# A kernel of convolution and 16 experts: the copy of a page's expert number moves to the head of VectorE's turn

## The chip, the core and the metric

The kernel runs on one core of a Trainium2 chip. The metric is the device time of one execution in microseconds; the time of a kernel is the median of its runs.

The engines are named as in the profile: PE is TensorE (matmuls; PEld its weight loads), DVE is VectorE, ACT is ScalarE, POOL is GpSimd, SP is SyncE, which here only issues DMAs. An engine's sequencer (ACTq, DVEq, SPq) handles what isn't work of the engine itself, such as loading a register from memory.

## The reference

Four sequences of 10048 positions with 128 channels go through a gated long convolution, and the 40192 rows that come out through one of 16 experts each, chosen in two steps (one group of four, then one of its four experts).

```
h = relu(pos_emb @ w1) @ w2 * exp(-0.01 * pos)          # the filter
y = irfft(rfft(x * v, 2*SEQ) * rfft(h, 2*SEQ))[:SEQ]    # a causal convolution of length SEQ
x = x * y                                               # 40192 rows of 128
g = argmax(x @ w_group);  e = argmax(x @ w_expert[g])   # weights: softmax over groups, over experts
out[row] = p_group * p_expert * (relu(x[row] @ w1[g, e]) @ w2[g, e])     # 128 -> 1024 -> 128
```

## The kernel before

The convolution stage takes the first 1,100 us or so, the routing of the rows follows, and the expert stage fills the second half of the execution, from 1250 us on. The change lies in the expert stage.

**Pages.** Routing sorts the rows into pages of 256, each of one expert, and `work` goes through 164 of them in a loop whose body is `turn`. Every matrix is split into a high and a low part (`wh` and `wl`, `xh` and `xl`, `hh` and `hl`), so that a product is three matmuls: high by high, high by low, low by high. The first weights `mw` of all experts stay in SBUF; the second ones, `ws`, come by two DMAs a page.

**A turn** works on five pages at once: it ends page `old`, does the second product of `p0` and the first of `p1`, transposes and splits the rows of `p2`, and begins `p3`, which means: find out its expert and fetch its second weights. The columns of 1024 are taken in blocks of 128, two to a relu, so the relus of a turn are those of blocks 0, 2, 4 and 6; the text calls them hh(0) to hh(6) on ScalarE and hl(0) to hl(6), the low parts, on VectorE. In the code `first(c)` (L1169 to L1171, into `ph`) and `second(c)` (L1188 to L1190, into `py`) are matmuls, `relu(c)` is hh (L1177) and hl (L1178), `high` and `low` are the casts of weights on ScalarE (L1150) and the subtractions on VectorE (L1158; for pages 2 to 41 one of the four is on GpSimd), `turn` of a page is the transpose `px` (L1130), `rows` makes `xh` and `xl`, `leave` copies `py` to `ys` (L1195), `turn_back` transposes it back, `ptm` (L1202), and `weigh` scales it into `os` (L1209).

**Order.** All these instructions are pinned: `k.fix` keeps each behind the one that the code wrote before it on the same engine. So the order of `turn` is the order of each engine. Not pinned are register loads (`value_load`) and the routing of the last batch, from which a step is taken every two turns; a scheduler puts these where it finds room.

**Beginning a page.** `begin` copies the page's expert number from the table `epgi` to a tile `ep` of one element (DVE, L1097), and three sequencers load it into a register: ScalarE's (L1099) and VectorE's (L1100), which address `mw` with it, and SyncE's (L1102), which addresses the two DMAs of `ws` (L1107). `ep` and `ws` have three buffers each.

**GpSimd's transfers.** `fetch` issues the gathers of a page's rows, `xg` (L1114, two a page, up to six pages ahead), the sends of finished rows, `out` (L1214, two a page, with up to 24 pages of `os` waiting), and the scatters of the last batch's list (L836). Lists are read back (`lst`, L1043) and turned into addresses on VectorE (`to` L1047, `of` L1049).

Of the kernel before, what the change touches and what calls it, by code (L numbers as in the profile page):

```python
# [14 lines left out]
I32 = mybir.dt.int32  # L15
# [115 lines left out]
class Kernel:  # L131
# [310 lines left out]
    def filter(self, ctx, ahead, made, folded):  # L442
# [35 lines left out]
        for k0, n in pairs + [(None, None)]:  # L478
            ahead_of, rest = rest, []
            if k0 is not None:  # L480
                o = k0 % 4
                if o == 0:
                    if k0 // 4 >= NBT:
                        bts.append(bp.tile([128, 4, 128], F32, tag="bt", name="bt", bufs=NBT))
                        m = min(4, NB - k0)
                        nc.sync.dma_start(bts[-1][:, :m], d["c_b"][:, k0 : k0 + m])
                    hs = tp.tile([128, 4, 2, 128], F32, tag="hs", name="hs", bufs=3)
                ps = self.dft_positions(k0, n, bts[k0 // 4][:, o:], k0 % 4 > 0)
                t = tp.tile([128, 2, 2, 128], F32, tag="hw", name="ht", bufs=4)


                for i in range(n):
                    cs, sn, mc = (phase[:, k0 + i, x : x + 1] for x in range(3))
                    tt, pp = t[:, i], ps[:, i]
                    whole = i == 0 or k0 % 8 == 0
                    if whole:
                        turn(nc.scalar.activation(tt[:, 0], pp[:, 0], AF.Copy, scale=cs))
                        turn(nc.scalar.activation(tt[:, 1], pp[:, 1], AF.Copy, scale=mc))
                    else:
                        turn(nc.scalar.activation(tt, pp, AF.Copy, scale=cs))  # L500
                    rest.append((whole, hs[:, o + i], pp, sn, tt))
                rest.append((k0, n, o, hs))
# [452 lines left out]
    def work(self, pages):  # L955


        n = len(pages)
        at = lambda i: pages[i] if 0 <= i < n else None
        for p in pages[:XG]:  # L960
            if p.xg is None:
                p.gather()
        if pages:
            pages[0].begin()
        for i in range(-2, n + 1):
            self.fetch(i, at(i + 1 + XG), at(i + 1))
            self.turn(at(i), at(i + 1), at(i + 2), at(i + 3), at(i - 1))
            if i >= 0 and i % EVERY == EVERY - 1:
                next(self.routing, None)
        while self.outs:  # L970
            self.outs.pop(0)()

    def turn(self, p0, p1, p2, p3, old):


        none = Idle()
        p0, p1, p2, p3, old = (p or none for p in (p0, p1, p2, p3, old))
        old.leave()
        p1.high(1, 0)
        p1.first(0)  # L980
        p2.turn()
        p0.second(0)
        p1.low(1, 0)
        p1.relu(0)
        p2.rows()
        p2.high(0, 0)
        old.turn_back()
        p0.second(1)
        p2.low(0, 0)
        old.weigh()  # L990
        p1.first(2)
        p0.second(2)
        p0.second(3)
        p1.relu(2)
        p2.high(0, 1)
        p1.high(1, 1)
        p2.low(0, 1)
        p1.low(1, 1)
        p1.first(4)
        p0.second(4)  # L1000
        p0.second(5)
        p1.relu(4)
        p3.begin()
        p1.first(6)
        p0.second(6)
        p0.second(7)
        p1.relu(6)
# [78 lines left out]
class Page:  # L1086
    def __init__(self, k, q):
        self.k, self.q = k, q
        self.to = self.of = self.weight = self.xg = None
        self.wh, self.wl, self.hh, self.hl, self.ph = ({}, {}), ({}, {}), [], [], {}  # L1090

    def begin(self):

        k, nc = self.k, self.k.nc
        ep = k.sp.tile([1, 1], I32, tag="ep", name="ep", bufs=3)
        k.tc.keep_in_program_order(
            nc.vector.tensor_copy(ep, k.pages.expert(self.q))  # L1097
        )
        self.ea = nc.scalar.value_load(ep, min_val=0, max_val=NE - 1)  # L1099
        self.ed = nc.vector.value_load(ep, min_val=0, max_val=NE - 1)  # L1100

        es = nc.sync.value_load(ep, min_val=0, max_val=NE - 1)  # L1102
        self.ws = []
        for half in range(2):
            ws = k.sp.tile([128, 512], F32, tag=f"ws{half}", name="ws", bufs=3)
            src = k.d["m_w2"][:, ds(es, 1), half * 512 : half * 512 + 512]
            k.tc.keep_in_program_order(nc.sync.dma_start(ws, src.rearrange("p e f -> p (e f)")))  # L1107
            self.ws.append(ws)
# [202 lines left out]
```

## Time and profile before

| | |
|---|---|
| median of 3 runs | 2534.3 us (2530.7 to 2542.32) |
| the profiled execution | 2529.75 us, span 2528.0 us |
| TensorE | 2053.1 us busy (81%), granted clock 0.912 in the mean |
| VectorE | 1719.8 us (68%) |
| GpSimd | 1500.5 us (59%) |
| ScalarE | 1347.5 us (53%) |
| turns 0 to 21 of the expert stage | 1261.3 to 1422.5 us |
| turns 22 to 31 | 1422.5 to 1593.8 us |
| turns 32 to 40 | 1593.8 to 1653.9 us |
| the 120 turns behind them | 1653.9 to 2501.3 us |

The shares are of the whole span and so mix stages with different limits. The profile counts the work of an engine as busy, not the work of its sequencer: a register load on ScalarE's sequencer holds back the next instruction of ScalarE, and shows there as idle time. Matmul durations overlap, so the distance between two starts, not the duration, is what a matmul costs. The granted clock is 1.00 at the full 2.4 GHz.

### The profile page before, as it was taken

How to read it: one execution, taken by the hardware profiler on the slowest of the kernel's cores; microseconds unless marked ns; L12 is line 12 of the kernel's file. 1: busy time of each engine (PE TensorE's matmuls, PEld its weight loads, DVE VectorE, ACT ScalarE, POOL GpSimd, SP SyncE). 2: the span in 40 equal slices, each digit the busy share in tenths (PEclk: the TensorE clock that was granted, in tenths of full speed). 3: DMA queues.
4: the chain of work that ended last, by engine and by line, in shares of the span. 5: the costliest groups of instructions: out<-in, count | busy, mean ns of one | idle time of the engine just before them, and what ended most of it. 6: DMA issues, size and time to landing. Idle time of an engine off the chain costs nothing.

```text
span 2528.0 us, 53511 instructions
## 1 busy us (share of the span) xinstructions
PE 2053.1 (81%) x18062; PEld 1846.6 (73%) x18062; DVE 1719.8 (68%) x3431; ACT 1347.5 (53%) x3005; POOL 1500.5 (59%) x1496
## 2 busy tenths in 40 slices
PE   9989899729996299813989655899999999999987
PEld 8778777607884187712788555888888888888887
DVE  5787778707797077911788623677777777777776
ACT  6733544305442054401677433677777777777776
POOL 2286016860596607674177777866666666666663
PEclk9999999859997599955999866999999999999999
DMA  4899568405773049521433211333333333333332
GB/s 130 296 271 273 148 202 278 126 9 135 252 234 108 10 140 300 166 62 40 152 109 111 74 49 40 111 117 110 113 113 114 114 113 114 114 113 109 111 109 69
DMA packets 201325, 338.65 MB, mean 134 GB/s; under 512 B 38558, under 2 KB 77185, under 8 KB 201040
## 3 DMA queue, kind: packets, MB, share of 16 engines
q1 hardware_dynamic: 159824, 275.64, 35.3%
q0 software_dynamic: 31712, 43.94, 5.6%
q10 hardware_dynamic: 9504, 15.54, 2.5%
q8 instruction: 146, 2.39, 0.4%
q14 instruction: 139, 1.14, 0.2%
HBM read 282.60 MB, written 53.30 MB: 133 GB/s over the span
## 4 chain that ended last, share of the span: by engine, by line
PE 33%; DVE 23%; issue 22%; ACT 8%; POOL 6%; DMA 4%; ACTq 3%; another core or an unknown queue 1%; SPq 0%; DVEq 0%; POOLq 0%
DVE wl L1158 7%; PE psa L301 4%; DVE hl L1178 3%; ACT wh L1150 3%; PE psb L371 3%; PE ph L1171 2%; DMA xv<-xv_in 2%; PE ph L1170 2%; PE ph L1169 2%; PE pbp L544 2%; ACTq L1099 2%; PE py L1190 2%; ACT ys L1195 2%; PE po L605 2%; PE py L1188 2%
## 5 line engine op out<-in xcount | busy, mean ns | idle before, releaser
L1178 DVE SCALAR_TENSOR_TENSOR hl<-ph,hh 128x512 fp32r<-128x512 f32 x656 | 451.1, 688 | 307.7 <-ACT hh L1177 262.4
L1177 ACT ACTIVATE hh<-ph 128x512 fp32r<-128x512 f32 x656 | 408.1, 622 | 364.6 <-PE px L1130 214.8
L1114 POOL DMA_INDIRECT xg<-xyd,of x328 | 388.6, 1185 | 229.9 <-PE px L1130 160.4
L1214 POOL DMA_INDIRECT out<-os,to x328 | 366.2, 1117 | 148.6 <-ACT os L1209 78.5
L1190 PE MATMUL py<-hh,wl 128*128 128x256 f32 x1312 | 378.5, 289 | 39.4 <-issue 27.0
L1188 PE MATMUL py<-hh,wh 128*128 128x256 f32 x1312 | 405.0, 309 | 0.3 <-issue 0.3
L836 POOL DMA_INDIRECT list<-en,adr x316 | 320.8, 1015 | 109.9 <-issue 88.3
L1169 PE MATMUL ph<-xh,wh 128*128 128x256 f32 x1312 | 377.9, 288 | 3.6 <-ACT xh L1137 2.6
L1170 PE MATMUL ph<-xl,wh 128*128 128x256 f32 x1312 | 377.6, 288 | 2.4 <-issue 2.4
L1171 PE MATMUL ph<-xh,wl 128*128 128x256 f32 x1312 | 377.6, 288 | 1.8 <-issue 1.4
L1189 PE MATMUL py<-hl,wh 128*128 128x256 f32 x1312 | 377.0, 287 | 1.0 <-issue 1.0
L533 POOL TENSOR_TENSOR y<-t 128x256 f32<-128x256 f32 (+1 forms) x160 | 119.4, 746 | 342.6 <-DVE t L532 340.0
L1190 PEld LDWEIGHTS py<-hh,wl 128*128 128x128 f32 x1312 | 257.2, 196 | 41.3 <-issue 28.4
L1169 PEld LDWEIGHTS ph<-xh,wh 128*128 128x128 f32 x1312 | 258.5, 197 | 4.4 <-ACT xh L1137 2.9
L1171 PEld LDWEIGHTS ph<-xh,wl 128*128 128x128 f32 x1312 | 257.8, 196 | 3.8 <-issue 2.9
L1189 PEld LDWEIGHTS py<-hl,wh 128*128 128x128 f32 x1312 | 258.3, 197 | 2.0 <-issue 2.0
L1170 PEld LDWEIGHTS ph<-xl,wh 128*128 128x128 f32 x1312 | 257.9, 197 | 0.7 <-issue 0.7
L1188 PEld LDWEIGHTS py<-hh,wh 128*128 128x128 f32 x1312 | 257.3, 196 | 1.1 <-issue 1.1
L1158 DVE TENSOR_TENSOR wl<-mw,wh 128x512 fp32r<-128x512 f32 x328 | 228.9, 698 | 0.3
L1150 ACT CAST wh<-ws 128x512 fp32r<-128x512 f32 x328 | 213.8, 652 | 12.6 <-remote 6.0
L1158 DVE TENSOR_TENSOR wl<-ws,wh 128x512 fp32r<-128x512 f32 x288 | 200.1, 695 | 23.0 <-ACT wh L1150 5.5
L1150 ACT CAST wh<-mw 128x512 fp32r x328 | 214.8, 655 | 0.0
(228 smaller groups left out, 4300.6 us busy)
## 6 DMA issues: line engine op xcount, KB each, us to landing
ws<-m_w SPq DMA_DIRECT2D x328, 256.0 KB
ht<-hspec SPq DMA_DIRECT2D x156, 256.0 KB
xv<-xv_in SPq DMA_DIRECT2D x131, 288.0 KB
bt<-c_b SPq DMA_DIRECT2D x95, 256.0 KB
bp<-c_bp SPq DMA_DIRECT2D x76, 256.0 KB
xyd<-xy SPq DMA_DIRECT2D x57, 256.0 KB
xo<-x_out ACTq DMA_DIRECT2D x60, 237.0 KB
hspec<-hs SPq DMA_DIRECT2D x19, 512.0 KB
```

The source lines that it names most:

```text
L1114: ins = nc.gpsimd.indirect_dma_start(self.xg[:, h], None, self.src, bass.IndirectOffsetOnAxis(ap=self.of[:, h : h + 1], axis=0), bounds_ch ...
L1150: k.fix(k.nc.scalar.copy(hi, self.matrix(i, half, self.ea)))
L1158: v.tensor_tensor(lo, self.matrix(i, half, self.ed), self.wh[i][half].bitcast(F32), ALU.subtract)
L1169: k.fix(nc.tensor.matmul(ph[:, j], wh, self.xh, start=True, stop=False))
L1170: k.fix(nc.tensor.matmul(ph[:, j], wh, self.xl, start=False, stop=False))
L1171: k.fix(nc.tensor.matmul(ph[:, j], wl, self.xh, start=False, stop=True))
L1177: k.fix(nc.scalar.activation(hh, ph, AF.Relu))
L1178: k.fix(nc.vector.scalar_tensor_tensor(hl, ph, 0.0, hh.bitcast(F32), ALU.max, ALU.subtract))
L1188: k.fix(nc.tensor.matmul(self.py, wh, self.hh[c], start=(c == 0), stop=False))
L1189: k.fix(nc.tensor.matmul(self.py, wh, self.hl[c], start=False, stop=False))
L1190: k.fix(nc.tensor.matmul(self.py, wl, self.hh[c], start=False, stop=(c == NC - 1)))
L1214: ins = k.nc.gpsimd.indirect_dma_start(k.d["out"], bass.IndirectOffsetOnAxis(ap=self.to[:, h : h + 1], axis=0), o[:, h], None, bounds_chec ...
```

## The change

`begin` is cut in two. The copy of the expert number becomes a function `number`, and `turn` calls it for `p3` ahead of everything else; the register loads and the DMAs of `ws` stay in `begin`, at its old place.

```diff
@@ work
         if pages:
+            pages[0].number()
             pages[0].begin()
@@ turn
         p0, p1, p2, p3, old = (p or none for p in (p0, p1, p2, p3, old))
+        p3.number()
         old.leave()
         p1.high(1, 0)
         p1.first(0)
@@ Page
+    def number(self):
+
+        k = self.k
+        self.ep = k.sp.tile([1, 1], I32, tag="ep", name="ep", bufs=3)
+        k.fix(k.nc.vector.tensor_copy(self.ep, k.pages.expert(self.q)))
+
     def begin(self):
 
-        k, nc = self.k, self.k.nc
-        ep = k.sp.tile([1, 1], I32, tag="ep", name="ep", bufs=3)
-        k.tc.keep_in_program_order(
-            nc.vector.tensor_copy(ep, k.pages.expert(self.q))
-        )
+        k, nc, ep = self.k, self.k.nc, self.ep
         self.ea = nc.scalar.value_load(ep, min_val=0, max_val=NE - 1)
         self.ed = nc.vector.value_load(ep, min_val=0, max_val=NE - 1)
```

On VectorE the order before reads so from hl(4) of a steady turn to hl(2) of the next turn:

```order
L1178 SCALAR_TENSOR_TENSOR hl<-ph,hh 128x512
L1097 COPY ep<-epgi_74 1x1
L1100 TENSOR_LOAD ep
L1100 ISA x2
L1178 SCALAR_TENSOR_TENSOR hl<-ph,hh 128x512
L1158 TENSOR_TENSOR wl_27341<-ws,wh_27325 128x512
L1178 SCALAR_TENSOR_TENSOR hl<-ph,hh 128x512
L1138 TENSOR_TENSOR xl<-px,xh 128x256
L1158 ISA
L1158 TENSOR_TENSOR wl_27359<-mw_11895,wh_27351 128x512
L1178 SCALAR_TENSOR_TENSOR hl<-ph,hh 128x512
```

and after the change, in another steady turn, where line numbers are 1 to 4 higher (the first row is hl(4) and hl(6) of the turn in one):

```order
L1162 TENSOR_TENSOR wl_28575<-ws,wh_28571 128x512
L1182 SCALAR_TENSOR_TENSOR hl<-ph,hh 128x512 x2
L1098 COPY ep<-epgi_74 1x1
L1162 TENSOR_TENSOR wl_28680<-ws,wh_28664 128x512
L1182 SCALAR_TENSOR_TENSOR hl<-ph,hh 128x512
L1142 TENSOR_TENSOR xl<-px,xh 128x256
L1162 ISA
L1162 TENSOR_TENSOR wl_28698<-mw_11895,wh_28690 128x512
L1104 TENSOR_LOAD ep
L1104 ISA x2
L1182 SCALAR_TENSOR_TENSOR hl<-ph,hh 128x512
```

The copy stood between hl(4) and hl(6); now it comes behind both, at the head of the next turn and for that turn's page. VectorE's register load (TENSOR_LOAD and two instructions for addresses, ISA) stood right behind the copy and stands now behind the first `wl` from `mw`. ScalarE's steady turn has one order before and after: the load stands behind hh(4) and ahead of hh(6).

On SyncE the load of the last part's list, `lst` with 380 elements, moves. Before, it follows the 33rd load of an expert number and that page's DMAs:

```order
L1102 TENSOR_LOAD ep
L1102 ISA x2
L1107 ISA
L1107 DMA ws<-m_w 128x512
L1107 ISA
L1107 DMA ws<-m_w 128x512
L1043 DMA lst_28642<-list 128x380
```

After the change it stands between the two weight loads of the 42nd:

```order
L1106 TENSOR_LOAD ep
L1106 ISA x2
L1111 ISA
L1111 DMA ws<-m_w 128x512
L1045 DMA lst_28642<-list 128x380
L1111 ISA
L1111 DMA ws<-m_w 128x512
```

With it move the scatters ahead of it: the 79 of the last batch on GpSimd end before the gathers of the 31st page in the order before, and before those of the 37th after; VectorE's two rows of `to` move from the 34th copy to the 42nd. TensorE's order is the same.

## Rows read from the trace of the kernel before

**Rows 1.** Windows of the expert stage: busy time per engine, clock, DMA share.

```profile
core 0: us, PE busy (x) PEld busy (x) DVE busy (x) ACT busy (x) POOL busy (x), PEclk, DMA share, GB/s
1261.30:1422.50 161.20, 142.75 (x1136) 139.35 (x1135) 141.18 (x279) 115.08 (x264) 121.54 (x107) 0.97 0.34 106
1422.50:1593.80 171.30, 91.41 (x523) 85.70 (x522) 53.26 (x95) 55.91 (x120) 134.16 (x130) 0.70 0.18 50
1593.80:1653.90 60.10, 56.49 (x460) 54.65 (x460) 44.50 (x82) 46.83 (x108) 50.30 (x46) 1.00 0.38 120
1653.90:2501.30 847.40, 770.85 (x6248) 746.25 (x6248) 655.89 (x1202) 625.52 (x1440) 552.91 (x472) 1.00 0.36 111
```

**Rows 2.** Tile `ep`, 1653.8 to 2501.4: count, duration (ns) min/median/max, first and last start.

```profile
L1097 DVE COPY ep<-epgi x121: 130/131/133, 1653.9 to 2501.3; 1x1 int32<-1x1 int32 x121
...
L1099 ACTq TENSOR_LOAD <-ep x120: 279/365/389, 1654.1 to 2494.5; - x120
```

**Rows 3.** View of waits, 1653.9 to 2501.3: total us, times, longest.

```profile
ACT hh L1177 <- PE px L1130: 202.5, 111, 2.1
```

**Rows 4.** Timeline of ScalarE in a steady turn: start, duration, then idle time before.

```profile
2000.18 0.60 ACT L1177 ACTIVATE hh<-ph 128x512 fp32r<-128x512 f32 x1 [1.82 <-PE px L1130]
...
2004.73 0.66 ACT L1177 ACTIVATE hh<-ph 128x512 fp32r<-128x512 f32 x1
2007.21 0.60 ACT L1177 ACTIVATE hh<-ph 128x512 fp32r<-128x512 f32 x1 [1.82 <-PE px L1130]
```

**Rows 5.** Timeline of TensorE at the same place.

```profile
2005.21 0.28 PE L1171 MATMUL ph<-xh,wl 128*128 128x256 f32 x1
...
2006.65 0.28 PE L1171 MATMUL ph<-xh,wl 128*128 128x256 f32 x1
2006.77 0.38 PE L1130 MATMUL px<-ident,xg 128*128 128x128 f32 x2
2006.91 0.37 PE L1188 MATMUL py<-hh,wh 128*128 128x256 f32 x1
...
2008.12 0.44 PE L1202 MATMUL ptm<-ident,ys 128*128 128x128 f32 x2 [0.61 <-ACT ys L1195]
```

**Rows 6.** Timeline of VectorE in that turn.

```profile
2000.81 0.69 DVE L1178 SCALAR_TENSOR_TENSOR hl<-ph,hh 128x512 fp32r<-128x512 f32 x1 [1.40 <-ACT hh L1177]
...
2006.31 0.13 DVE L1097 COPY ep<-epgi 1x1 int32<-1x1 int32 x1
2007.84 0.69 DVE L1178 SCALAR_TENSOR_TENSOR hl<-ph,hh 128x512 fp32r<-128x512 f32 x1 [1.40 <-ACT hh L1177]
```

**Rows 7.** Timeline of ScalarE in the turn that begins no page.

```profile
2506.77 1.39 ACT L1177 ACTIVATE hh<-ph 128x512 fp32r<-128x512 f32 x2
```

**Rows 8.** Timeline of TensorE in that turn: its first transpose and the next turn's.

```profile
2503.13 0.44 PE L1202 MATMUL ptm<-ident,ys 128*128 128x128 f32 x2 [0.58 <-ACT ys L1195]
...
2509.16 0.38 PE L1202 MATMUL ptm<-ident,ys 128*128 128x128 f32 x2
```

**Rows 9.** VectorE's sequencer by line L1100 (ns), and VectorE's timeline, around 1306.

```profile
L1100 DVEq TENSOR_LOAD <-ep x1: 304/304/304, 1305.9 to 1305.9; - x1
...
1305.80 0.67 DVE L1158 TENSOR_TENSOR wl<-ws,wh 128x512 fp32r<-128x512 f32 x1
```

**Rows 10.** Timeline of GpSimd in a steady turn.

```profile
2000.40 1.04 POOL L1114 DMA_INDIRECT xg<-xyd,of  x1 [1.36 <-PE px L1130]
2001.75 1.43 POOL L1114 DMA_INDIRECT xg<-xyd,of  x1 [0.30 <-issue]
2003.49 1.23 POOL L1214 DMA_INDIRECT out<-os,to  x1 [0.30 <-ACT os L1209]
2005.02 1.04 POOL L1214 DMA_INDIRECT out<-os,to  x1 [0.30 <-ACT wh L1150]
```

**Rows 11.** Tile `ep`, 1261.2 to 1653.8: who waited for it (us, times).

```profile
  ACT hh L1177: 20.4, 5
```

**Rows 12.** Windows of the convolution stage, columns as in Rows 1.

```profile
272.00:302.70 30.70, 27.10 (x408) 24.07 (x406) 24.96 (x50) 15.93 (x28) 0.00 (x0) 1.00 0.54 141
302.70:306.10 3.40, 3.40 (x38) 2.79 (x36) 1.91 (x6) 0.55 (x1) 0.00 (x0) 0.50 0.80 207
```

## The prediction

> **What bounds the kernel now.** I read the table of windows first, to split the expert stage where its behaviour changes [rows 1]. A turn is told by its copy of the expert number, so the 121 copies from 1653.9 to 2501.3 bound 120 turns [rows 2]: 847.4 us, 7.06 us a turn. TensorE is busy for 770.85 us of them (91%), VectorE 77%, ScalarE 74%, GpSimd 65%. No engine is full, so something makes them wait for each other. The view of waits says where: a relu on ScalarE waits 111 times, 202.5 us in all, 1.8 us each [rows 3]. The view puts it down to TensorE's transpose into `px`. That name has to be tested.
>
> ScalarE's timeline shows one such wait. The turn's third relu, hh(4), starts at 2004.73 and ends at 2005.39; the fourth, hh(6), starts at 2007.21 after 1.82 us of idle time [rows 4]. On TensorE the last matmul of `first(6)`, which hh(6) reads, starts at 2005.21 and ends at 2005.49; from there to the `px` pair at 2006.77 come six `py` and six `ph` steps of others [rows 5]. So TensorE had been done with hh(6)'s input for 1.7 us. What ends just before 2007.21 is another chain. VectorE copies the expert number at 2006.31 and is done at 2006.44 [rows 6]. ScalarE's sequencer then loads it into a register, 0.365 us by the median [rows 2], and works out addresses, and 0.77 us after the copy's end hh(6) starts. ScalarE is in order, so hh(6), the copy `ys` and the next `wh` stand behind that load.
>
> The loop closes in two places. Late `ys` leaves TensorE idle for 0.61 us before the transposes `ptm` [rows 5]. Late hh(6) leaves VectorE idle for 1.40 us before its low part [rows 6]; VectorE then runs its ten steps in order, and the tenth is the next copy. Copy, load, hh(6), VectorE's row of work, copy: this ring sets the turn, 7.03 us from one hh(6) to the next (2000.18 to 2007.21) [rows 4].
>
> The trace holds one turn without copy and load, the one that has no page left to begin. There hh(4) and hh(6) run back to back (one row of two, 1.39 us, no idle time) [rows 7], and the transposes `ptm` stand 6.03 us apart (2503.13 to 2509.16), the second of them with no idle time ahead [rows 8]. That is the kernel's own answer to most of the question.
>
> **The change, part by part.** Nothing is added or removed: one copy, three register loads and two weight loads a page, as before. What moves in a steady turn is the copy, from behind hl(4) to the head of VectorE's turn, and VectorE's own register load, from the copy to behind the first `wl` from `mw`. ScalarE's and TensorE's order stay.
>
> *ScalarE's load.* It stands between hh(4) and hh(6) as before, but its number is there some 5 us earlier. ScalarE has 5.21 us of work from 2000.18 to 2005.39 [rows 4]; with the load wholly uncovered, 0.77 us, that makes 5.98. This is below what TensorE needs, so I cost the load at nothing. Its cover is hh(4) and the wait for the matmuls of hh(6).
>
> *TensorE's floor.* A turn has 48 matmuls at 0.12 us and two pairs of transposes at 0.14 us [rows 5]: 6.04 us. The turn without a load took 6.03 us, but it had no `px` pair; adding 0.14 gives 6.17 as the upper end (part of it is a slow start after an idle stretch). I take 6.10, between the two. Saving: 7.03 - 6.10 = 0.93 us a turn, 112 us for 120 turns; the ends are 103 and 119. What 847.4 has over 120 x 7.03, 4 us, is left as it is.
>
> *VectorE.* From 2000.81 to the copy's end at 2006.44 it takes 5.63 us, small gaps included [rows 6]. Its own load now follows a `wl`. An earlier place of the trace shows such a load beside a running `wl`: it starts at 1305.9 and takes 0.304 us, while `wl` runs from 1305.80 for 0.67 [rows 9]. Covered, it costs nothing; uncovered, at ScalarE's 0.77, VectorE's turn would be 6.40 us and the saving 76 us. I take the covered case, since the row is of the same two operations.
>
> *SyncE* has the number earlier, so the two weight loads of a page are issued earlier; they have three buffers, and the view of waits names no engine that waits for them in the steady turns. I cost it at nothing.
>
> *GpSimd* becomes the closest follower. A steady turn has two gathers and two sends, 1.04, 1.43, 1.23 and 1.04 us, with 0.30 us of issue ahead of each [rows 10]: 4.74 + 1.20 = 5.94 us, against 6.04 to 6.17. It fits, with little room.
>
> *The first 41 turns.* The routing of the last batch and its list scatters on GpSimd lie here, and the change spreads them over later turns. From 1422.5 to 1593.8 GpSimd is busy for 134.16 us with 130 instructions [rows 1]; 0.30 us of issue for each makes it 173 us in a stretch of 171.3: full. From 1593.8 to 1653.9 it is busy for 50.30 us; 0.30 us ahead of each of four DMAs in nine turns makes it 61 in a stretch of 60.1: full too, at 6.68 us a turn. An earlier copy gives nothing to a full GpSimd. In the 22 turns before them, 161.2 us, 6.68 each would make 147; the 14 us over that come from routing work on VectorE (141.18 us busy), and part of it reaches ScalarE through the copy, since hh waits for `ep` 20.4 us in five places before 1653.8 [rows 11]. Bounds: 0 and 14; I take 5, since VectorE still has all that routing to do and only the copy no longer stands behind it.
>
> *Sum.* 2529.75 - 112 - 5 = 2413 for an execution like the profiled one. The median of the runs is 4.55 us above that one: 2417.
>
> **A rule that speaks against it.** GpSimd's DMAs are of two lengths: a turn's second gather takes 1.43 us, the first 1.04 [rows 10]. A shorter turn packs VectorE's work more closely around all four. The Trainium skill, page "SBUF — State Buffer", section "SBUF: two separate sides", warns of this: while VectorE runs a copy that holds the port pair it shares with GpSimd, the descriptors of a DMA issued from GpSimd's queue can't be written. By the rows the sum stays 2417; by that rule, with each of the four of the long kind, GpSimd would set the turn and little would be saved (the first rival has the price). The trace agrees in part only: VectorE's idle time in a turn is the 1.40 us that end at 2007.84, so the last send, from 2005.02 to 2006.06, ran beside a busy VectorE and still took the short 1.04.
>
> **Rivals.** *GpSimd takes the place of the wait.* With three DMAs at 1.43 and one at 1.04 a turn is 5.33 + 1.20 = 6.53 us: 60 us saved, 2469. With all four it is 6.92: 13 us, 2516. For it: 5.94 is only 0.1 below the floor. Against it: six pages of gathered rows and 24 of weighed ones are kept, so that one long DMA delays nobody, and the last send was short beside a busy VectorE. Chance 0.14.
>
> *TensorE's clock gives some back.* In the steady turns it is 1.00 with TensorE busy 91% [rows 1]. In an earlier stage it was 1.00 from 272.0 to 302.7 with TensorE busy 88%, then 0.50 for the next 3.4 us [rows 12]. If a fuller turn met that pattern, a tenth of 120 x 6.10 = 732 us would run at half speed: 732/0.95 = 770, 38 us back, 2455. Chance 0.09.
>
> *Slower than before*, by one mechanism: that clock at a worse share. With a share s at 0.50 (1.2 in place of 2.4 GHz) a turn takes 6.10/(1 - s/2). It is back at 7.03 for s = 0.26; from s = 0.29 the kernel is over 0.5% slower (12.7 us, about what a measurement here can tell from none): 2547 and more. Against it: the strongest pattern in the rows is a share of 0.10. Chance 0.04.
>
> *It doesn't do what it says.* If the wait were TensorE's after all, as the view of waits has it, or another took its whole place, the time would stay within 12.7 us of 2534. Against it stands the turn without a load. Chance 0.05.
>
> **How the numbers follow.** The forecast has 0.68; its own range is 2400 to 2432 (119 and 14 us saved, or 103 and nothing). Faster by over 0.5%: forecast, GpSimd and the mild clock, 0.91; within 0.5%: 0.05; slower: 0.04. From 2400 to 2470 lie nearly all of the forecast, the mild clock, VectorE's uncovered load (2453) and the gentler part of GpSimd's case, some 0.8.
>
> **What would show it.** Right: steady turns of 6.04 to 6.17 us by the copies; hh(6) behind hh(4) with under 0.8 us of idle time; no wait of `ptm` for `ys`; TensorE busy over 97% there; the first 41 turns changed by less than 15 us. Wrong: GpSimd's gaps down to the 0.30 of issue in all steady turns (it binds); a clock under 1.00 there; VectorE idle behind its own load; a long wait for the last list, whose address work now stands behind the 42nd copy on VectorE.

## The result, and the profile after

The changed kernel takes 2472.56 us (median of 4 runs, 2459.73 to 2478.78) against 2532.89 us of the kernel before (4 runs beside it): ratio 0.9751, 95% interval 0.9722 to 0.9781. It is 60 us faster where the forecast was 117, and lies 2.6 us above the stated range. The profiled execution took 2471.89 us, 57.9 less than the one of before, with a span of 2470.1.

The page after, its busy line and the first line of its chain, and behind them that line of the chain in the page before:

```profile
PE 2036.5 (82%) x18062; PEld 1843.2 (75%) x18062; DVE 1737.3 (70%) x3431; ACT 1370.0 (55%) x3005; POOL 1477.8 (60%) x1496
...
PE 35%; issue 3%; another core or an unknown queue 2%; ACT 1%; DVE 0%; ACTq 0%; POOL 0%; DVEq 0%; POOLq 0%
```

```profile
PE 33%; DVE 23%; issue 22%; ACT 8%; POOL 6%; DMA 4%; ACTq 3%; another core or an unknown queue 1%; SPq 0%; DVEq 0%; POOLq 0%
```

In the chain after, VectorE's row of work and ScalarE's sequencer (ACTq) round to 0%; what is left is TensorE. The shares of this chain add up to 41%, since it could be followed back only through the last 1,020 us or so, most of which are the steady turns; the one before reaches through the whole span. The copy no longer marks the turns evenly, so I count turns by the transposes `ptm`: two to a turn, 242 rows for 120 turns and the pair that closes the last one. The steady part after, as a window and by the tile `ptm`:

```profile
1659.40:2445.20 785.80, 755.68 (x6249) 744.46 (x6249) 660.75 (x1200) 642.43 (x1442) 531.38 (x471) 1.00 0.39 120
```

```profile
L1206 PE MATMUL ptm<-ident,ys x242: 270/273/331, 1659.5 to 2445.0; 128*128 128x128 f32 x121
```

From 1659.5 to 2445.0 are 785.5 us, 6.55 a turn; before, 847.4 [rows 1, 2]. So the steady turns gave 62 us. TensorE is busy 96%; the prediction's sign was over 97%. The first 40 turns, up to the start of that window, became no faster: `ptm` runs from 1269.3 to 1659.6 here, 390.3 us; in the trace before, from 1269.5 to 1655.8, 386.3 us.

The view of waits over those steady turns says what is left:

```profile
ACT hh L1181 <- PE ph L1175: 48.1, 61, 2.3
...
PE ptm L1206 <- ACT ys L1199: 27.7, 36, 1.7
...
ACT hh L1181 <- PE py L1194: 24.3, 35, 2.0
ACT hh L1181 <- PE px L1134: 17.6, 24, 2.3
```

Two kinds of turn are mixed. In a regular one no `ptm` waits: the TensorE timeline has pairs 6.20 us apart, with nothing between them but work.

```profile
1719.69 0.38 PE L1206 MATMUL ptm<-ident,ys 128*128 128x128 f32 x2
1719.83 0.36 PE L1192 MATMUL py<-hh,wh 128*128 128x256 f32 x1
1720.03 0.28 PE L1193 MATMUL py<-hl,wh 128*128 128x256 f32 x1
...
1725.89 0.38 PE L1206 MATMUL ptm<-ident,ys 128*128 128x128 f32 x2
```

The pair costs 0.14 us as in [rows 5], but the matmul behind it starts the next one 0.20 later, not 0.12. Two pairs a turn make 0.16 us that my floor of 6.04 lacked. The trace before had it too: the matmul behind `px` starts at 2006.91 [rows 5], and the next one 0.20 us later.

```profile
2007.11 0.28 PE L1189 MATMUL py<-hl,wh 128*128 128x256 f32 x1
```

The other kind of turn is longer: 50 of the 120 take over 6.3 us from pair to pair, the longest 8.37, and the view has 36 waits of `ptm` for `ys`, up to 1.7 us. Here is ScalarE's timeline through both kinds, a regular turn (1722 to 1725) and a long one (1735 to 1739); what TensorE had done by then stands in the next fence.

```profile
1722.71 0.60 ACT L1181 ACTIVATE hh<-ph 128x512 fp32r<-128x512 f32 x1
1724.18 0.60 ACT L1181 ACTIVATE hh<-ph 128x512 fp32r<-128x512 f32 x1 [0.87 <-PE ph L1175]
...
1735.90 0.60 ACT L1181 ACTIVATE hh<-ph 128x512 fp32r<-128x512 f32 x1 [0.71 <-PE ph L1175]
1738.08 0.60 ACT L1181 ACTIVATE hh<-ph 128x512 fp32r<-128x512 f32 x1 [1.59 <-PE px L1134]
1738.58 0.37 ACT L1199 COPY ys<-py 128x256 f32<-128x256 f32 x1
```

The last matmul of `first(4)` in either turn, the last of `first(6)` in the long one, and the transposes behind it:

```profile
1722.31 0.28 PE L1175 MATMUL ph<-xh,wl 128*128 128x256 f32 x1
...
1734.69 0.28 PE L1175 MATMUL ph<-xh,wl 128*128 128x256 f32 x1
...
1736.13 0.28 PE L1175 MATMUL ph<-xh,wl 128*128 128x256 f32 x1
...
1739.00 0.44 PE L1206 MATMUL ptm<-ident,ys 128*128 128x128 f32 x2 [0.58 <-ACT ys L1199]
```

In the regular turn `first(4)` ends at 1722.59 and hh(4) starts 0.12 us later. In the long turn it ends at 1734.97 and hh(4) starts 0.93 later; `first(6)` ends at 1736.41 and hh(6) starts 1.67 later. ScalarE was idle for 0.71 and 1.59 us of that. The register load still stands between the two relus, but it is not what hh(6) waits for. It starts right behind hh(4)'s start,

```profile
L1103 ACTq TENSOR_LOAD <-ep x1: 279/279/279, 1735.9 to 1735.9; - x1
```

and by the same trace its address work is over at 1736.46, before hh(4) ends at 1736.50. So TensorE's results were there (by the record) and the signal came late. (In the regular turn `first(6)` ends at 1724.03 and hh(6) starts 0.15 us later; its 0.87 us of idle time are a little over the 0.8 of the prediction's sign.) A relu that starts 1.67 us late makes `ys` late, and TensorE stops, here for 0.58 us.

### The profile page after: what moved, and what is told of

It reads as the page before. It is cut to its first block, busy times and chain, and to the rows that moved or that the text cites. A ratio compares the mean times of both kernels' runs of the same rounds, so it can differ in the third digit from the quotient of the medians.

```text
span 2470.1 us, 53512 instructions
## 1 busy us (share of the span) xinstructions
PE 2036.5 (82%) x18062; PEld 1843.2 (75%) x18062; DVE 1737.3 (70%) x3431; ACT 1370.0 (55%) x3005; POOL 1477.8 (60%) x1496
## 5 line engine op out<-in xcount | busy, mean ns | idle before, releaser
L1181 ACT ACTIVATE hh<-ph 128x512 fp32r<-128x512 f32 x656 | 398.7, 609 | 235.4 <-PE ph L1175 75.3
L1118 POOL DMA_INDIRECT xg<-xyd,of x328 | 382.4, 1166 | 189.0 <-PE px L1134 114.9
L1218 POOL DMA_INDIRECT out<-os,to x328 | 354.5, 1081 | 139.3 <-issue 54.0
L1162 DVE TENSOR_TENSOR wl<-ws,wh 128x512 fp32r<-128x512 f32 x288 | 209.4, 727 | 43.1 <-ACT wh L1154 18.8
L301 PE MATMUL psa<-fa,eo 96*64 96x158 f32 x2048 | 188.6, 317 | 40.2 <-issue 32.8
```

The costliest lines, as they stand in the source:

```text
L1118: ins = nc.gpsimd.indirect_dma_start(self.xg[:, h], None, self.src, bass.IndirectOffsetOnAxis(ap=self.of[:, h : h + 1], axis=0), bounds_ch ...
L1162: v.tensor_tensor(lo, self.matrix(i, half, self.ed), self.wh[i][half].bitcast(F32), ALU.subtract)
L1181: k.fix(nc.scalar.activation(hh, ph, AF.Relu))
L1218: ins = k.nc.gpsimd.indirect_dma_start(k.d["out"], bass.IndirectOffsetOnAxis(ap=self.to[:, h : h + 1], axis=0), o[:, h], None, bounds_chec ...
```

## Experiments

The experiments met two kinds of chip. The record numbers four: on one the kernel before takes 2315.84 us, on the other three 2536.54 to 2545.39, much as in the runs of the prediction (2532.89). I compare with the kernel before on the same chip, and call the two kinds the quicker chip and the slower chips.

**The two halves of the change, and a later `ptm` (quicker chip).** In `steady_only` the copy comes first for pages from 46 on, in `early_only` for pages below 46; elsewhere it stays at its old place.

```diff
-        p3.number()
+        if p3 is not none and p3.q >= 46:      # early_only: < 46
+            p3.number()
...
+        if p3 is not none and p3.q < 46:       # early_only: >= 46
+            p3.number()
         p3.begin()
```

> The copy comes first only for pages 46 and later; for pages 0 to 45 it stands at its old place, and the routing and the list load lie where they lay before the change. If the early turns gain nothing from the change because GpSimd is full there: 2465 to 2475, the changed kernel's time. If the shift of routing and lists to later turns costs something that hides an early gain: 2455 to 2465. If the early copy itself gains there: 2480.

> The copy comes first only for pages 0 to 45; the steady turns are as before the change. If the whole gain is that of the steady turns: 2530 to 2540, within 0.3% of the kernel before, and steady turns of 7.02 us. If the early turns carry part of the gain: 2515 to 2525.

`late_ptm` is the changed kernel with

```diff
-        old.turn_back()
         p0.second(1)
         p2.low(0, 0)
-        old.weigh()
         p1.first(2)
+        old.turn_back()
...
         p1.relu(2)
+        old.weigh()
```

> The changed kernel with one more move: the two transposes ptm of the page that ends stand behind first(2) on TensorE, nine matmuls (1.08 us) later than now, and the scaling os behind hh(2) on ScalarE. Theory 1 (TensorE's signals come late when it streams without a pause, and ys is then late for ptm): 1.08 us more of slack swallow most of the long turns, whose surplus is 41.5 us in the 120 steady turns; steady turns 6.2 to 6.3 us in the mean, time 2430 to 2445 us. Theory 2 (GpSimd, at about 6 us a turn, sets the long turns): the transposes' place changes nothing, mean 6.5 us, time 2465 to 2480.

Measured, against 2315.84: `steady_only` 2216.96 (ratio 0.9579, 0.9559 to 0.9599), `early_only` 2303.55 (0.9943, 0.9927 to 0.9958), `late_ptm` 2205.91 (0.9526, 0.9512 to 0.9541). The steady turns by the tile `ptm`, in this order:

```profile
L1209 PE MATMUL ptm<-ident,ys x242: 270/272/330, 1443.8 to 2188.1; 128*128 128x128 f32 x121
```

```profile
L1209 PE MATMUL ptm<-ident,ys x242: 270/273/330, 1434.9 to 2277.2; 128*128 128x128 f32 x121
```

```profile
L1206 PE MATMUL ptm<-ident,ys x242: 270/271/273, 1435.5 to 2177.8; 128*128 128x128 f32 x121
```

These are 6.20, 7.02 and 6.19 us a turn. On this chip the steady turns gain 98.9 us, and the move of `ptm` gains nothing there, since `ptm` hardly waits in `steady_only` by the view of waits. TensorE is busy for 743.62 of its 744.30 us, so the load holds nothing up. The first line is that of the waits, the second the window:

```profile
PE ptm L1209 <- ACT ys L1202: 0.9, 2, 0.7
```

```profile
1443.80:2188.10 744.30, 743.62 (x6246) 742.90 (x6247) 655.51 (x1203) 638.32 (x1442) 541.01 (x470) 1.00 0.41 127
```

The early copy gains 12.3 us; its first 40 turns are 376.9 us long (1058.1 to 1435.0) against 387.6 of `steady_only` (1056.4 to 1444.0). The halves add up to 111 us of the 117 forecast. My expectations for the times themselves missed: they were written for a slower chip. The changed kernel itself has no run on the quicker one.

**Which chip, which cause (a slower chip).** The changed kernel again, the later `ptm` again, the changed kernel without copy and loads from page 46 on, and without the sends.

> The changed kernel, unaltered, beside the kernel before on whatever chip this call gets. On a chip where the kernel before takes about 2316 us and TensorE's signals come on time, as in the runs above: no long turns, 120 steady turns of 6.19 us, ratio 0.952 to 0.957 (105 us for the steady turns and some 5 for the early ones). On a chip where the kernel before takes about 2533 us: ratio 0.975, 40 to 50 long turns. If the long turns belong to the change itself (register load, GpSimd) and not to the chip: long turns, and a ratio above 0.97, on either chip.

> The changed kernel with the transposes ptm nine matmuls later and os behind hh(2). Where TensorE's signals come on time: 0 to 4 us off the changed kernel, since no ptm waits there. On a chip with late signals (the kernel before at about 2533 us): 25 to 40 us off the changed kernel, long turns with a surplus of at most 15 us in place of 41.

```diff
# no_loads: Page.number returns at once, and ea, ed and es are the constant 0, for q >= 46
+        if self.q >= 46:
+            return
...
# no_sends: Page.weigh
+        if self.q < 46:
+            k.outs += [lambda h=h: self.send(o, h) for h in range(TH)]
```

> The changed kernel without the copy and the three register loads from page 46 on; expert 0 is used for all these pages, so their results are left out of account. If the load is wholly hidden after the change: steady turns as in the changed kernel to 0.02 us, time within 3 us of it. If the load or its address work still costs: 0.1 us a turn and more, 12 us and more faster.

> The changed kernel without the sends of finished rows from page 46 on (two of GpSimd's four DMAs a turn, whose rows are left out). If GpSimd does not bind: steady turns of the same length to 0.03 us, and as many long turns as the changed kernel has on the same chip. If GpSimd's 5.9 us a turn set the 6.19: turns of 6.0 to 6.1 us, 10 us and more faster.

Measured against 2540.47: `after_again` 2478.09 (ratio 0.9748, 0.9730 to 0.9765), `late_ptm_again` 2459.65 (0.9693, 0.9666 to 0.9719), `no_loads` 2477.58 (0.9758, 0.9735 to 0.9780), `no_sends` 2434.27 (0.9581, 0.9555 to 0.9606). The steady turns of the four, in this order:

```profile
L1206 PE MATMUL ptm<-ident,ys x242: 270/272/330, 1659.5 to 2453.8; 128*128 128x128 f32 x121
```

```profile
L1206 PE MATMUL ptm<-ident,ys x242: 270/272/330, 1648.5 to 2425.8; 128*128 128x128 f32 x121
```

```profile
L1209 PE MATMUL ptm<-ident,ys x242: 270/273/330, 1655.4 to 2445.6; 128*128 128x128 f32 x121
```

```profile
L1206 PE MATMUL ptm<-ident,ys x242: 270/272/476, 1664.5 to 2414.6; 128*128 128x128 f32 x121
```

That is 6.62, 6.48, 6.59 and 6.25 us a turn. Without any load the turns are in the mean as long as with it, so the long turns aren't its doing. They are mixed in another way, though: in `after_again` 47 of the 120 turns take over 6.3 us, up to 9.24, in `no_loads` 111, up to 7.76, and there a relu waits in nearly every turn:

```profile
ACT hh L1184 <- PE py L1197: 118.1, 102, 1.5
```

So that the load itself costs nothing is shown by `steady_only` on the quicker chip rather than by this mean. Without the sends nearly all long turns vanish (3 of 120 are over 6.3 us) and the kernel is 44 us faster than `after_again`, where my expectation had such a gain only with turns of 6.0 to 6.1 us. The later `ptm` takes 18 us off, less than I expected.

**Writing or issuing?** A send is work for GpSimd and a write to memory outside the core. Two kernels part these. In `gather_for_send` each send from page 46 on is one more gather into the same `os` tile (no rows are written); in `sp_sends` plain DMAs of SyncE's queue write the same bytes to consecutive rows.

```diff
# gather_for_send: Page.send, q >= 46
+            ins = k.nc.gpsimd.indirect_dma_start(o[:, h], None, self.src,
+                bass.IndirectOffsetOnAxis(ap=self.of[:, h : h + 1], axis=0), ...)
# sp_sends: Page.send, q >= 46
+            r = (self.q - 46) * TP + h * 128
+            ins = k.nc.sync.dma_start(k.d["out"][r : r + 128], o[:, h])
```

> The changed kernel, but from page 46 on each send of finished rows is replaced by one more gather into the same os tile, with the same wait for os; these rows are not written out. GpSimd issues as many indirect DMAs as before, but in these turns none writes to memory outside the chip's SBUF. On a chip where the kernel before takes about 2535 us: if the sends' writes are what delays TensorE's signals, there are few long turns (surplus under 15 us, time 2430 to 2445 us); if it is GpSimd's work of issuing four indirect DMAs a turn, they stay (surplus 35 us and more, time 2465 to 2485). Where the kernel before takes about 2316 us, no long turns either way, 2200 to 2212 us.

> The changed kernel, but from page 46 on the finished rows of a page are written by two plain DMAs of SyncE's queue to consecutive rows of the output, which is not their right place. The same bytes are written, GpSimd issues only the two gathers. On a chip where the kernel before takes about 2535 us: if the writes delay TensorE's signals, the long turns stay (surplus 35 us and more, 2465 to 2485); if GpSimd's issuing of scattered sends does, few are left (surplus under 15 us, 2430 to 2445 us). Where the kernel before takes about 2316 us, no long turns either way, 2200 to 2212 us.

Measured against 2545.39 (a slower chip): 2487.61 (0.9784, 0.9745 to 0.9823) and 2432.72 (0.9566, 0.9525 to 0.9606). The view of waits of the first, and of the second:

```profile
PE ptm L1206 <- ACT ys L1199: 35.2, 46, 1.8
```

```profile
PE ptm L1206 <- ACT ys L1199: 2.1, 4, 0.9
```

Their turns are 6.70 us (1655.9 to 2459.5) and 6.22 us (1669.7 to 2416.4). The first lies 3 us above what I had expected for the case of GpSimd's issuing, the second inside it. The bytes written don't matter, and the number of DMA packets doesn't either: from 1700 to 2400 us there are 71914 in `sp_sends` and 44576 in the profile after. That GpSimd issues four indirect DMAs a turn in place of two does. Whether they must be indirect wasn't tried.

**Less for TensorE, and a still later `ptm`.** `thin_pe` leaves the eight matmuls of hl by `wh` out of the changed kernel from page 46 on; it ran on either kind of chip. `later_ptm` (a slower chip) has `ptm` behind `second(3)` and `os` behind the second `wh` from `ws`.

```diff
# thin_pe: Page.second
+        if self.q < 46:
+            k.fix(nc.tensor.matmul(self.py, wh, self.hl[c], start=False, stop=False))
# later_ptm, against late_ptm
         p1.first(2)
-        old.turn_back()
         p0.second(2)
         p0.second(3)
+        old.turn_back()
         p1.relu(2)
-        old.weigh()
         p2.high(0, 1)
         p1.high(1, 1)
+        old.weigh()
```

> The changed kernel without the matmuls of hl by wh (eight of 48 a turn) from page 46 on, so a part of the second product is left out: TensorE's floor falls by 0.96 us to 5.2 us and it must pause in every turn. Theory 1: the signals come on time, turns are regular, their length is that of the next engine, 5.6 to 6.0 us (GpSimd 5.9 or VectorE 5.6), with hardly a long turn, time 2385 to 2410. Theory 2 (GpSimd at over 6 us): mean of 6.4 to 6.5 us as in the changed kernel, 2460 to 2475.

> The changed kernel without the matmuls of hl by wh from page 46 on (their part of the result is left out), so that TensorE needs 5.2 us a turn and pauses in it, with all four GpSimd DMAs. On a chip where the kernel before takes about 2540 us: if late signals need both GpSimd's four DMAs and a TensorE without pauses, turns of 5.4 to 5.8 us as on the other chip, 2360 to 2385 us. If GpSimd's DMAs delay signals whatever TensorE does, or if GpSimd's 5.9 us a turn bind: turns of 6.0 us and more, above 2400.

> As the kernel with the later transposes, but ptm stands behind second(3) on TensorE, 15 matmuls (1.8 us) later than in the changed kernel, and os behind the second wh from ws on ScalarE. On a chip where the kernel before takes about 2540 us: if the long turns are ys being late for ptm, another 0.7 us of slack takes some 10 to 20 us more than the 18 us that the first step took, 2440 to 2452 us; if they are any wait for a late signal, ptm only being the first to meet it, nothing more is gained, 2455 to 2465. Where the kernel before takes about 2316 us: 2203 to 2209 us.

On the quicker chip `thin_pe` took 2143.83 us (ratio 0.9256, 0.9238 to 0.9273), on a slower one 2475.85 (0.9769, 0.9736 to 0.9801). The same work, by the tile `ptm`, first on the quicker, then on the slower chip, and last the slower chip's window:

```profile
L1207 PE MATMUL ptm<-ident,ys x242: 270/271/275, 1431.9 to 2114.2; 128*128 128x128 f32 x121
```

```profile
L1207 PE MATMUL ptm<-ident,ys x242: 269/272/477, 1649.4 to 2450.7; 128*128 128x128 f32 x121
```

```profile
1649.40:2450.90 801.50, 695.03 (x5328) 677.54 (x5327) 653.05 (x1200) 639.67 (x1442) 528.94 (x473) 0.94 0.39 118
```

These are 5.69 and 6.68 us a turn. So GpSimd's four DMAs don't limit a turn to 5.9 us on the quicker chip, and on the slower one the turn is no shorter with a sixth of TensorE's work gone. The granted clock explains only a part of that: it is 0.94 in this stretch, and TensorE is busy for 695.03 us where it needs 651.67 on the quicker chip at 1.00. With all of these 43 us taken off, 6.32 us a turn are left (an estimate). That refutes my guess that signals come late only where TensorE streams without a pause. `later_ptm` took 2462.47 (0.9712, 0.9688 to 0.9737, against 2536.54): nothing beyond `late_ptm`. More slack for `ys` alone doesn't help, as expected for the case that any relu can meet a late signal.

**What the late signals go with.** The trace holds the arrivals of the semaphore through which TensorE signals. In the steady turns on the quicker chip every arrival follows the end of a matmul that signals by less than 0.02 us. I call an arrival off the beat when no such matmul ended in the 0.02 us before it. Each profile has 1201 matmuls that signal there; on the slower chips some 120 to 200 of their arrivals are missing from the record, so the counts there are rough.

| kernel | chip | arrivals | off the beat |
|---|---|---|---|
| `early_only`, `steady_only`, `late_ptm`, `thin_pe` | quicker | 1199 to 1201 | 0 |
| the kernel before | slower | 1057 | 49 |
| the changed kernel, and `after_again` | slower | 1049, 1071 | 493, 523 |
| `no_loads` | slower | 1063 | 448 |
| `late_ptm_again`, `later_ptm` | slower | 1028, 1013 | 465, 676 |
| `thin_pe_again` | slower | 1057 | 519 |
| `gather_for_send` | slower | 1004 | 484 |
| `no_sends`, `sp_sends` | slower | 1080, 1074 | 22, 38 |

In the long turn shown above, matmuls that signal end at 1736.41, 1737.13, 1737.85, 1737.96 and 1738.07; the arrivals come in one bunch, at 1738.06, 1738.14, 1738.21, 1738.25 and 1738.28.

Late signals keep to the rows of GpSimd's DMAs. In the profile after, 228 matmuls signalled more than 0.45 us after GpSimd's last DMA had ended, and none of these signals was over 0.2 us late. Of 311 that ended 2.5 to 5 us into a row without such a pause 109 were not, 163 were, and for 39 the record is missing. But a row alone is not enough. In the trace of the kernel before 298 of 320 such matmuls were on time, and it has 103 rows of four DMAs or more where the profile after has 94. And GpSimd's timeline has the same row of four in the regular turn (from 1719.76) as in the long one (from 1732.32):

```profile
1719.76 1.36 POOL L1118 DMA_INDIRECT xg<-xyd,of  x1 [1.37 <-PE px L1134]
1721.42 1.19 POOL L1118 DMA_INDIRECT xg<-xyd,of  x1 [0.30 <-issue]
1722.92 1.08 POOL L1218 DMA_INDIRECT out<-os,to  x1 [0.31 <-ACT wh L1154]
1724.31 1.01 POOL L1218 DMA_INDIRECT out<-os,to  x1 [0.30 <-issue]
...
1732.32 1.20 POOL L1118 DMA_INDIRECT xg<-xyd,of  x1 [0.65 <-PE px L1134]
1733.82 1.20 POOL L1118 DMA_INDIRECT xg<-xyd,of  x1 [0.30 <-issue]
1735.32 1.06 POOL L1218 DMA_INDIRECT out<-os,to  x1 [0.30 <-ACT wh L1154]
1736.68 1.00 POOL L1218 DMA_INDIRECT out<-os,to  x1 [0.30 <-issue]
1738.54 1.04 POOL L1118 DMA_INDIRECT xg<-xyd,of  x1 [0.86 <-PE px L1134]
```

`first(4)` ends 2.83 us into the first row, and hh(4) follows 0.12 us later; it ends 2.65 us into the second, and hh(4) follows 0.93 later. hh(6) starts at 1738.08, 0.40 us after the end of the second row. What makes one row hold signals up and another not isn't shown.

## Why the prediction was right, and where it was wrong

**The wait and its ring: right.** ScalarE's load set the steady turns; with the copy at the head they fall from 7.02 to 6.20 us wherever signals come on time (`steady_only`, and the regular turns of the profile after). That the load then costs nothing is shown by TensorE's 743.62 busy us of 744.30 in `steady_only`; taking it out on a slower chip gained nothing either (`no_loads`). The view of waits had named TensorE's `px` for that wait; the turn without a load was the better witness.

**TensorE's floor: 0.1 us too low.** I took 6.10; it is 6.20, because the matmul behind each pair of transposes costs 0.20 and not 0.12, as the trace before already had it. Over 120 turns that is 12 us of the 59 by which the profiled execution (2471.89) missed the sum (2413).

**GpSimd: the step that failed.** I wrote "It fits, with little room" and priced it at nothing. By length it does fit, and nothing waits for GpSimd's data. But in the shorter turn, on the slower chips, TensorE's signals come late as long as GpSimd issues four DMAs a turn: 493 of 1049 arrivals are off the beat, where the longer turn before has 49 of 1057, and 22 and 38 are left with two DMAs a turn. The long turns cost 785.5 - 120 x 6.20 = 41.5 us, and `no_sends` takes 44 us off. With the 0.1 us of the floor that is the whole difference in the steady turns: 112 - 12 - 41.5 = 58.5, measured 62; the rest is about the 4 us that the sum had left as they are. The 9 us that are still lacking of the 59 are those of the early turns, where 5 us of gain were forecast and 4 were lost (386.3 to 390.3).

The first rival gave 2469, but it came close to the time by luck. It has GpSimd's DMAs getting longer, and that is refuted: in the steady turns the gathers and sends have means of 1169 and 1093 ns after the change, and had 1218 and 1132 ns before. The Trainium skill, page "SBUF — State Buffer", section "SBUF: two separate sides", says that GpSimd can't write a DMA's descriptors while VectorE runs an operation that takes the port pair of both, such as a copy. I had expected longer DMAs from that, with VectorE busier (84% after, 77% before). The trace doesn't show them, and the only copy in VectorE's steady turn is that of the expert number, 0.131 us long.

**The early turns: 5 us forecast.** By the tile `ptm` the first 19 of them gained 7.7 us in the profile after (140.3 to 132.6) and 9.7 on the quicker chip (140.8 in `steady_only`, 131.1 in `early_only`). In the 21 behind them, where GpSimd's scatters run one after the other, the quicker chip gained 0.9 us and the slower one lost 11.8 (245.8 to 257.6; the nine profiles with the early copy on slower chips have 250.9 to 259.2). So the gain was there and somewhat larger than forecast, that a full GpSimd gives none was right, and the loss was not foreseen. Signals are late in these turns in either kernel, 103 of 178 arrivals off the beat before and 114 of 188 after, and none of 210 on the quicker chip; why the scatters' new place costs time on the slower chips alone wasn't tried.

**The clock, VectorE's own load, the list: nothing.** The granted clock of the steady part is 1.00, as before, with TensorE at 96%. The prediction's strongest pattern, a share of 0.10 at the lower clock, was that of a stretch with TensorE busy; [rows 1] also have a clock of 0.70 from 1422.5 to 1593.8, with TensorE busy 53%. VectorE's load is covered: in the regular turn it and its address work run from 1720.8 to 1721.4, while `wl` runs until 1721.72, and hl(2) starts at 1721.82. VectorE waits for the lists for 5.7 us in all, and did so for 11.6 before.

**A faster version.** `late_ptm`, the later transposes on top of the change, beats both kernels on a slower chip: it has 0.9693 of the time before, and the change alone has 0.9748. On the quicker chip it has 0.9526; the change alone wasn't run there.

**Open.** How GpSimd's issuing holds up the signals isn't shown, only that halving it, with the same bytes written, all but ends it. Nor is it known why the kernel before, with as many rows of four DMAs, has hardly any late signal in its steady turns, or why the slower chips have them and the quicker one doesn't.

## What to carry to other kernels

When a wait is named after an engine that had long been done, follow the waiting engine's own sequencer: a register load of a number that another engine makes last is a link in a ring, and making the number early cost nothing here. When such a ring opens, the turn gets shorter for every engine, and what the longer turn left room for, here late signals of TensorE beside GpSimd's DMAs, shows up as irregular turns, so look at the spread of the turns and not at their mean alone. Before a number of such size is trusted, run it on a second chip.

## What the hardware showed that I had not expected

On the slower chips signals of TensorE come late within rows of GpSimd's indirect DMAs, by 1.65 us in the turn shown; on the quicker one `thin_pe` issues them at 5.69 us a turn, with three pauses of over 0.45 us in its 120 turns, and no arrival is off the beat. Something that may or may not be the same stands in the routing of the convolution stage of the kernel before, where TensorE's transposes crawl beside the list scatters. First TensorE, then GpSimd at the same time, then the window around them:

```profile
533.51 0.37 PE L564 MATMUL pt<-ident,z 128*32 128x128 f32 x1 [2.43 <-issue]
534.91 0.13 PEld L564 LDWEIGHTS pt<-ident,z 128*32 128x32 f32 x1 [2.67 <-issue]
536.31 0.37 PE L564 MATMUL pt<-ident,z 128*32 128x128 f32 x1 [2.43 <-issue]
```

```profile
533.47 0.99 POOL L836 DMA_INDIRECT list<-en,adr  x1 [0.30 <-issue]
534.76 0.98 POOL L836 DMA_INDIRECT list<-en,adr  x1 [0.30 <-issue]
536.05 0.98 POOL L836 DMA_INDIRECT list<-en,adr  x1 [0.31 <-issue]
```

```profile
517.00:565.00 48.00, 7.28 (x20) 2.63 (x20) 1.29 (x2) 0.55 (x1) 35.16 (x36) 0.50 0.02 1
```

A weight load or a matmul starts every 1.40 us, and no wait is named; here it is not a signal that is late, but TensorE's next instruction that doesn't start. The granted clock is 0.50 in this stretch, with TensorE busy for 7.28 of 48 us. Between 517 and 565 us TensorE sat idle for 40.1 us in all ahead of these transposes (20 of them); on the quicker chip the same line of `late_ptm` has 216 in a stretch of 120 us, with 55 list scatters beside them and no idle time. The idle time lies on the chain that ended last, so it is part of the 217 us by which the kernel before is quicker on that chip. It differs from run to run, though: over the whole execution it is 43.6 us ahead of this line in the trace before, and 14.9 in the one after.
